# An attention and mixture-of-experts kernel: gathered rows turned on VectorE in 32x32 blocks by way of DRAM, and VectorE's sums in another order

## The chip, the cores and the metric

One core of a Trainium2 chip, all in fp32. A core has a tensor engine (TensorE, PE: matmuls and transposes, results in PSUM), a vector engine (VectorE, DVE), a scalar engine (ScalarE, ACT), GpSimd (POOL) and SyncE (SP); the last issues most DMAs here. The metric is the device time of one execution in microseconds (us), the median of the runs. For one execution there is a profile, which gives the time of every instruction on each engine and of the DMAs.

## The reference

Linear attention with decay over 4 sequences of 768 tokens and 8 heads of 64 gives a row `x` of 512 numbers for each token. Then a mixture of experts with a rule of locality: a token goes to its own best expert, or stays with the expert of the token before it.

```python
def _moe_ref(x, w_gate, w_local, w1, w2):
    B, S, D = x.shape                      # 4, 768, 512; 8 experts, F = 1024
    logits = np.einsum('bsd,de->bse', x, w_gate)
    local_gate = 1.0 / (1.0 + np.exp(-np.einsum('bsd,de->bse', x, w_local).squeeze(-1)))
    for b in range(B):
        prev_e = -1
        for s in range(S):
            fresh_e = int(np.argmax(logits[b, s]))
            if s == 0 or local_gate[b, s] < 0.5:
                e = fresh_e
            else:
                e = prev_e if prev_e >= 0 else fresh_e
            prev_e = e
            ...
            h = np.maximum(x[b, s] @ w1[e], 0.0)
            out[b, s] = p[e] * (h @ w2[e])
```

Only the expert that a token goes to is computed: per token a product of 512 by 512x1024, a relu, and a product of 1024 by 1024x512, scaled by the gate's probability.

## The kernel before

**Stages.** The attention runs in 24 steps of 128 rows; each writes its rows of `x` to `x_dram` in DRAM and the gate's logits to SBUF. DVE, PE and POOL work out which token goes to which expert and sort the tokens by expert into tiles of up to 128 tokens, each tile of one expert. The first `KA` = 5 tiles are made early, from the sequences that are done, so that they keep PE busy while the rest is sorted. What is left is done in three kinds: pairs (two full tiles of one expert), single tiles (`full`) and half tiles of 64 tokens. How many there are of each is known only as the kernel runs: `while_more` and `one_of` branch on it. In the profiled execution there are 8 pairs, 3 single tiles after the first 5, and 3 half tiles. The order is: pair 0, pair 1 (the half tiles' steps stand in these two as hooks), pair 2, the single tiles, then pairs 3 to 7.

**Rows.** `collect` gathers a tile's rows from `x_dram` into `xgt[i]` (i = 0, 1; token on the partition, 512 numbers in a row) by an indirect DMA of POOL. A product needs them the other way round, the 512 on the partitions in four groups of 128. `turned` does that: four transposes on PE (L666) into the PSUM bank `po1`, and a copy out of it, by ACT into `xp` for a pair, by DVE into `xtt[i]` for a single tile.

**Single and half tiles.** `hidden` (L674) makes the hidden layer, `output` (L680) the second product, `written` scales by the gate on DVE and scatters the rows to the output with POOL (L689).

**Pairs.** `pair` multiplies two tiles as a 2x2 block product with seven products per layer in place of eight (Strassen's scheme in Winograd's form). `product_1` (L863) is a product of layer 1, `product_2` (L868) one of layer 2. The scheme needs sums of blocks, all on DVE: `sums_of_x` over the turned rows (into `xs` and `xp`), `sums_1` over w1 (into `s1`, and one block of w1 in place), `sums_2` over w2 (into `s2`, and one block in place), four instructions each; the sums of products are in `part` (`c01`, `c10`, `c11`) for layer 1 and in `yt` and `rest` for layer 2. Products go to PSUM banks `a`, `b`, `c`; in layer 2 `c` is `pl`, and is used twice: for `hs[2]`, which the second sum of `c11` (L942) reads, and then for `h00`.

A pair prepares the next: it gathers the next pair's rows at its start (`pair_ahead`), turns the first tile after the second product of layer 2 and the second one after the fourth, adds up w1 of the next pair beside that, and makes `sums_of_x` after the sixth product. `hook(k)` calls what the caller puts between the products.

**Weights.** There are three sets in SBUF, `w1t[i]` and `w2t[i]` of 2 MB each. Pair p uses set (p+1) % 2, the half tiles set 2, the single tiles set 2 and set 1 in turn. `weights_of` loads w1 (L636) and w2 (L638) of a tile's expert by one DMA each on SP's queue; a pair loads w1 of the pair after next at its middle (after hook 6) and w2 at its end, into the set that it used itself. Before pair 2 both layers of the first single tile are loaded into set 2. The DMAs of one engine are issued in the order of its program, and a DMA that waits (for the last reader of the buffer, or a semaphore) holds up those behind it.

**Order.** In the shown part, PE, DVE and SP run in the order in which the code calls them (`manual_schedule`); ACT's and POOL's order is made by the scheduler.

Of the kernel before, what the change touches and what calls it, by code (L numbers as in the profile page):

```python
# [8 lines left out]
F32 = mybir.dt.float32  # L9
# [12 lines left out]
P = 128  # L22
# [21 lines left out]

HP = P // 2
REST = N - KA * P
PMIN = -(-(REST - E * (P + HP)) // (2 * P))
# [12 lines left out]
def kernel(  # L60
# [16 lines left out]
    dram = ctx.enter_context(tc.tile_pool(name="dram", bufs=1, space=bass.MemoryType.DRAM))  # L77
    x_dram = dram.tile([N, DM], F32, name="x_dram")
    lt = route.tile([P, NT, E + 1], F32, name="lt")
    moe = ctx.enter_context(tc.tile_pool(name="moe", bufs=2))  # L80
# [169 lines left out]
    def rows_of(s):  # L250
        px = pg.tile([P, DM], F32, name="pk1")
        for a in range(A):
            nc.tensor.transpose(px[:, P * a:P * a + P], xc[:, a, ORDER[s][0]], ident)
        if s + 1 < NS:
            xn = att.tile([P, DM], F32, name="xn", bufs=4)
        else:
            xn = act.tile([P, DM], F32, name="xn", bufs=1)
        nc.scalar.copy(xn, px)
        nc.scalar.dma_start(out=x_dram[P * s:P * s + P, :], in_=xn)
# [372 lines left out]

    def weights_of(g, i, layers=(1, 2), cond=None):
        e = expert(g)
        if 1 in layers:
            nc.sync.dma_start(out=w1t[i], in_=w1_src(e), cond=cond, cond_hint=None if cond is None else True)  # L636
        if 2 in layers:
            nc.sync.dma_start(out=w2t[i], in_=w2_src(e), cond=cond, cond_hint=None if cond is None else True)  # L638
# [76 lines left out]
    with tc.manual_schedule(engines={PE, DVE, SP}):  # L715
# [57 lines left out]
        xgh = act.tile([P, DM], F32, name="xgh", bufs=1)  # L773
        yt = act.tile([P, 2, DM], F32, name="y", bufs=1)
        xp = act.tile([P, DT, 2, P], F32, name="xp", bufs=1)
        xs = act.tile([P, 3, DT // 2, P], F32, name="xs", bufs=1)
# [89 lines left out]
    def product_2(to, a, b, new=False):  # L866
        for f in range(FT // 2):
            nc.tensor.matmul(to, lhsT=a[:, f], rhs=b[:, f], start=(new and not f), stop=(f == FT // 2 - 1),  # L868
                             skip_group_check=True)

    def pair_ahead(p):
        for i in range(2):
            ahead(KA + 2 * p + i, i)

    def pair_turned(i):
        turned(i, xp[:, :, i], nc.scalar.copy)

    def pair(p, hooks={}, next=True, load=True, cond=None):
# [12 lines left out]
        product_1(a, a1(p, 0, 0), b1(0, 0), True)  # L891
        nc.scalar.copy(c01, a)
        hook(0)
        product_1(b, s1[:, 1], xs[:, 1], True)
        tt(c10, c01, b, ALU.add)  # L895
        hook(1)
        sums_2(p, (0, 1))
        product_1(c, a1(p, 1, 0), b1(0, 1), True)
# [3 lines left out]
        tt(c11, c11, c, ALU.add)  # L902
        nc.scalar.activation(h11, c11, ACT.Relu)
        hook(3)
        sums_2(p, (2, 3))
        product_1(a, a1(p, 0, 1), b1(1, 0))
# [12 lines left out]
        nc.scalar.activation(h01, c01, ACT.Relu)  # L919
        hook(6)  # L920
        if load:
            weights_of(KA + 2 * p + 4, w_of(p), (1,), cond)
# [6 lines left out]
        nc.scalar.mul(c01, a, g1)  # L929
        hook(7)  # L930
        product_2(b, hs[:, 1], s2[:, 1], True)
        tt(hs[:, 3], h01, hs[:, 1], sub)
        stt(c10, b, g0, rest, ALU.mult, ALU.add)
        hook(8)
        if next:
            pair_turned(0)
            sums_1(p + 1, (0, 1))
        product_2(c, hs[:, 2], b2(p, 0, 1), True)
        hook(9)
        product_2(b, hs[:, 0], s2[:, 0])  # L940
        stt(c11, b, g0, rest, ALU.mult, ALU.add)
        stt(c11, c, g0, c11, ALU.mult, ALU.add)  # L942
        hook(10)
        if next:
            pair_turned(1)
            sums_1(p + 1, (2, 3))
        product_2(a, h01, b2(p, 1, 0))
        nc.scalar.mul(c00, a, g1)
        hook(11)
        product_2(c, h00, s2[:, 2])  # L950
        stt(c10, c, g0, c10, ALU.mult, ALU.add)  # L951
        scatter(KA + 2 * p, yt[:, 0])
        if next:
            sums_of_x()
        hook(12)
# [11 lines left out]
    def turned_half():  # L967
# [4 lines left out]
        nc.vector.tensor_copy(xt, pt[:, :, :HP])  # L972
        return xt

    def hidden_of_half(xt):
# [31 lines left out]
    def hooks_of_halves(n):  # L1007
# [7 lines left out]
        def steps(h):  # L1015
# [11 lines left out]
            def end():  # L1027
                output_of_half(h, now["ht"])
                if h + 1 < n:
                    weights_of(G2 + h + 1, 2)  # L1030

# [29 lines left out]
    with tc.manual_schedule(engines={PE, DVE, SP}):  # L1061
# [6 lines left out]
        hidden(0, 0, 0)  # L1068
        hidden(0, 0, 1)
        weights_of(KA + 2, w_of(1), (1,))  # L1070
        pair_turned(0)
        sums_1(0, range(4))
        output(0, 0)
        pair_turned(1)
        sums_of_x()
        written(4, 0)
        weights_of(KA + 2, w_of(1), (2,))
        weights_of(G2, 2)

# [7 lines left out]
        fulls = number(1, E + 1)  # L1087
        pair(2, {10: [lambda: ahead(G1, 0)], 12: [lambda: ahead(G1 + 1, 1)], 13: [lambda: turned(0)]}, load=False)

# [3 lines left out]
        def full(f):  # L1093

            i, w = f % 2, w_of_full(f)
            if f + 1 < E:
                if f:
                    ahead(G1 + f + 1, 1 - i)
                else:
                    weights_of(G1 + 1, w_of_full(1), cond=fulls > 1)  # L1100
            hidden(i, w, 0)
            hidden(i, w, 1)
            if f + 1 < E:
                turned(1 - i)
            output(i, w)
            written(G1 + f, i)
            if f + 2 < E:
                weights_of(G1 + f + 2, w, cond=fulls > f + 2)

# [46 lines left out]
```

## Time and profile before

| | us |
|---|---|
| runs | 478.14, 480.98, 483.45; median 480.98 |
| the profiled execution | 479.6 |
| its span, from the first instruction to the last | 477.9 |
| mean granted TensorE clock | 0.989 |

Stages of the profiled execution, in us from the start of the span:

| stretch | what | PE busy | DVE busy |
|---|---|---|---|
| 0 to 170 | attention, sorting, first tiles | 159.7 | 95.8 |
| 170 to 184 | the last of the first five tiles | 14.0 of 14 | 6.0 |
| 184 to 264 | pairs 0 and 1 with the half tiles | 76.9 of 80 | 42.5 |
| 264 to 290 | pair 2 | 26.0 of 26 | 19.7 |
| 290 to 338 | three single tiles | 43.8 of 48 | 5.3 |
| 338 to 478 | pairs 3 to 7 | 127.6 of 140 | 95.7 |

Pairs 3 to 7 start at 338.33, 364.0, 389.5, 415.0 and 440.5. An engine's name with a q (SPq) is the queue that issues for it. In a line of the timeline or the chain the first number is the start, the second the duration; `x8` counts instructions. The releaser of a wait is what came last by the semaphores.

### The profile page before, as it was taken

The page shows a single profiled execution, that of the slowest core. Times are in us where ns is not written, and L with a number is a line of the kernel's source. Part 1 is how long each engine was busy: PE and PEld are TensorE (multiplying, and loading weights), DVE is VectorE, ACT ScalarE, POOL GpSimd, SP SyncE. Part 2 cuts the span into 40 slices and gives each one's busy share as a digit, 9 for nine tenths or more (in the row PEclk, how much of TensorE's full clock was granted, in tenths as well). Part 3 has the DMA queues.
Part 4 walks back from the last instruction along what each step waited for, and adds up shares of the span by engine and source line. Part 5 has one row for each costly group of instructions (what it writes and reads, how often), then busy time and mean ns, then how long its engine had stood idle before and what let it go on. Part 6 is the DMA issues. An engine that isn't in the chain of part 4 may idle for free. (4 is left out here: it accounts for less than half of the span.)

```text
span 477.9 us, 10471 instructions
## 1 busy us (share of the span) xinstructions
PE 447.9 (94%) x4307; PEld 371.4 (78%) x4307; DVE 264.9 (55%) x515; ACT 112.4 (24%) x265; POOL 112.9 (24%) x121
## 2 busy tenths in 40 slices
PE   8898999999999998899999999989999999999990
PEld 7776887777776776868777988647799999998980
DVE  6553676762269451835473783101386868687780
ACT  3265665431100110211121130000031312121120
POOL 4574654500111200214001311101203030110200
PEclk9899999999999999999999999999999999999997
DMA  7999999996888988998990799831594838250201
GB/s 289 406 421 350 364 346 344 394 408 230 282 306 300 359 278 302 403 394 314 347 352 12 239 360 405 308 132 41 185 392 156 299 91 317 93 205 23 67 3 46
DMA packets 42241, 126.20 MB, mean 264 GB/s; under 512 B 3132, under 2 KB 3132, under 8 KB 39360
## 3 DMA queue, kind: packets, MB, share of 16 engines
q1 hardware_dynamic: 34256, 104.88, 59.7%
q0 software_dynamic: 4464, 14.16, 8.1%
q10 hardware_dynamic: 3456, 6.29, 3.5%
q8 instruction: 40, 0.66, 0.5%
q14 instruction: 25, 0.20, 0.1%
HBM read 137.91 MB, written 12.98 MB: 316 GB/s over the span
## 5 line engine op out<-in xcount | busy, mean ns | idle before, releaser
L689 POOL DMA_INDIRECT out_dram<-y,sidx x24 | 24.8, 1034 | 199.6 <-DVE y L951 98.9
L674 PEld LDWEIGHTS ps<-xt,w 128*128 128x128 f32 x512 | 58.1, 192 | 4.5 <-issue 2.6
L674 PE MATMUL ps<-xt,w 128*128 128x128 f32 x512 | 59.2, 276 | 1.3 <-DVE xt L667 1.0
L680 PE MATMUL pk<-w,h 128*128 128x512 f32 x128 | 56.3, 592 | 0.0
L651 POOL DMA_INDIRECT xg<-x_dram,gidx x27 | 30.5, 1130 | 77.7 <-PE po L666 36.8
L680 PEld LDWEIGHTS pk<-w,h 128*128 128x128 f32 x128 | 23.7, 190 | 26.8 <-issue 26.8
L198 DVE TENSOR_TENSOR sm<-ps,mask 128x512 f32<-128x512 f32 x46 | 29.6, 686 | 20.4 <-PE ps L194 20.4
L863 PE MATMUL ps<-xp,w 128*128 128x128 f32 x256 | 31.7, 276 | 2.6 <-issue 1.5
L863 PEld LDWEIGHTS ps<-xp,w 128*128 128x128 f32 x256 | 30.4, 192 | 4.5 <-issue 4.2
L863 PE MATMUL ps<-xs,s 128*128 128x128 f32 x256 | 31.3, 275 | 1.6 <-DVE part L895 1.6
L676 ACT ACTIVATE h<-ps 128x512 f32<-128x512 f32 x16 | 9.6, 597 | 94.1 <-PE ps L674 74.7
L863 PEld LDWEIGHTS ps<-xs,s 128*128 128x128 f32 x256 | 29.9, 192 | 1.8 <-DVE part L895 1.8
L169 POOL TENSOR_TENSOR qd<-inp,lamq 128x512 f32<-128x512 f32 x20 | 25.6, 1281 | 20.2 <-PE po L221 8.8
L868 PE MATMUL pk<-w,h 128*128 128x256 f32 x128 | 30.3, 379 | 0.0
L868 PE MATMUL pk<-s,hsum 128*128 128x256 f32 x128 | 30.2, 379 | 0.0
L234 PE MATMUL po<-sm,inp 128*64 128x128 f32 x384 | 27.5, 284 | 1.2 <-issue 1.1
L234 PEld LDWEIGHTS po<-sm,inp 128*64 128x64 f32 x384 | 21.3, 139 | 8.1 <-issue 6.9
L868 PEld LDWEIGHTS pk<-s,hsum 128*128 128x128 f32 x128 | 24.0, 190 | 3.1
L172 POOL TENSOR_TENSOR kd<-inp,rev 128x512 f32<-128x512 f32 x20 | 21.7, 1084 | 19.6 <-PE pk L243 10.1
L868 PEld LDWEIGHTS pk<-w,h 128*128 128x128 f32 x128 | 23.1, 190 | 2.5
L697 DVE TENSOR_SCALAR y<-pk,gate 128x512 f32<-128x512 f32 x8 | 6.0, 748 | 33.1 <-PE pk L680 27.1
L194 PE MATMUL ps<-inp 64*64 64x128 f32 (+1 forms) x736 | 21.4, 253 | 3.0 <-DMA inp<-in_qkv_dram 1.8
(244 smaller groups left out, 734.1 us busy)
## 6 DMA issues: line engine op xcount, KB each, us to landing
w<-in_w_dram SPq DMA_DIRECT2D x49, 2048.0 KB
inp<-in_qkv_dram SPq DMA_DIRECT2D x22, 1024.0 KB
x_dram<-xn ACTq DMA_DIRECT2D x24, 256.0 KB
inp<-in_qkv_dram SPq DMA_DIRECT2D x4, 512.0 KB
w<-in_w_dram SPq DMA_DIRECT2D x4, 512.0 KB
xg<-x_dram,gidx POOLq DMA_INDIRECT x27, 6.7
out_dram<-y,sidx POOLq DMA_INDIRECT x24, 6.9
xgh<-x_dram,gidx POOLq DMA_INDIRECT x3
```

The source lines that it names most:

```text
L169: nc.gpsimd.tensor_tensor(qd, x[:, 0].rearrange("p (a i) -> p a i", i=P), lamq, ALU.mult)
L172: nc.gpsimd.tensor_tensor(kd.rearrange("p (h d) -> p h d", d=DH), x[:, 2].rearrange("p (h d) -> p h d", d=DH), rev.unsqueeze(2).broadcast_ ...
L194: nc.tensor.matmul(ps[u][half, a, first:], lhsT=kt[rows, a, js], rhs=qt[rows, a, first:], start=True, stop=True, skip_group_check=True)
L198: nc.vector.tensor_tensor(sm[:, u], ps[u], mask[:, u], ALU.mult)
L234: nc.tensor.matmul(head(a, u), lhsT=vn[:, a, u], rhs=sm[:, u, a], start=(not c and a < 2), stop=True, skip_group_check=True)
L651: nc.gpsimd.indirect_dma_start(out=xg, out_offset=None, in_=x_dram[:n, :], in_offset=bass.IndirectOffsetOnAxis(ap=gidx[i][:, j:j + 1], axi ...
L674: nc.tensor.matmul(ph[:, j], lhsT=w1t[w][:, d, P * f:P * f + P], rhs=xtt[i][:, d], start=(d == 0), stop=(d == DT - 1))
L676: nc.scalar.activation(hq[half, i], ph, ACT.Relu)
L680: nc.tensor.matmul(pys[i], lhsT=hq[f // 4, i][:, f % 4], rhs=w2t[w][:, f], start=(f == 0), stop=(f == FT - 1))
L689: apart(nc.gpsimd.indirect_dma_start(out=out, out_offset=bass.IndirectOffsetOnAxis(ap=sidx[i][:, j:j + 1], axis=0), in_=y, in_offset=None, ...
L863: nc.tensor.matmul(to[:, m], lhsT=a[:, k, P * m:P * m + P], rhs=b[:, k], start=(new and not m and not k), stop=(k == 1), skip_group_check= ...
L868: nc.tensor.matmul(to, lhsT=a[:, f], rhs=b[:, f], start=(new and not f), stop=(f == FT // 2 - 1), skip_group_check=True)
```

## The change

- The gathered rows of pairs and single tiles are not turned on PE any more. SP writes `xgt[i]` to a buffer in DRAM (`xg_dram[i]`, 256 KB) and reads it back in four DMAs of 64 KB (`fetched`): quarter q of each row goes to the partitions 32q to 32q+31, with four groups of 32 tokens side by side. One transpose on DVE then turns every 32x32 block in place (`blocks_turned`). A row's element on partition 32q+j, group d, is thus number 128q + 32d + j; before, partition p of group d held number 128d + p.
- w1 has to lie in the same order. `weights_of` therefore loads w1 by four DMAs, one for each 32 partitions (0.5 MB each). Half tiles keep the turns on PE and the old order (`weights_of_half`). The first five tiles keep both too.
- In a pair, `sums_2` stands earlier (for pair 0 in one row after `c11`), the first two of `sums_1` of the next pair stand in layer 1, the last two after the first and second product of layer 2 (in pair 0 two and two there), both turns after the third, and `sums_of_x` after the fifth. The writes and reads of the next pair's rows are issued after hook 6, ahead of the load of w1.
- In pair 2 the rows of two single tiles are gathered at hook 7. A single tile turns the next one's rows at its start, gathers those of the one after next there, and fetches them at its end.
- The last step's `xn` takes a part of `part` as its buffer, so that there is room for the two tiles `xqs`.

Line numbers of the file after the change are higher by 4 at `weights_of` and by about 50 at its end.

```diff
@@ -76,6 +78,8 @@
 
     dram = ctx.enter_context(tc.tile_pool(name="dram", bufs=1, space=bass.MemoryType.DRAM))
     x_dram = dram.tile([N, DM], F32, name="x_dram")
+
+    xg_dram = [dram.tile([P, DM], F32, name=f"xg_dram{i}") for i in range(2)]
     lt = route.tile([P, NT, E + 1], F32, name="lt")
     moe = ctx.enter_context(tc.tile_pool(name="moe", bufs=2))
     rt = ctx.enter_context(tc.tile_pool(name="rt", bufs=1))
@@ -631,9 +635,13 @@
         nc.sync.dma_start(out=w2t[g % 2], in_=w2_src(e), cond=other, cond_hint=False)
 
     def weights_of(g, i, layers=(1, 2), cond=None):
+
         e = expert(g)
         if 1 in layers:
-            nc.sync.dma_start(out=w1t[i], in_=w1_src(e), cond=cond, cond_hint=None if cond is None else True)
+            rows = w1[bass.ds(e, 1)].rearrange("o (q t j) f -> q j (o t) f", q=Q, j=QP)
+            for q in range(Q):
+                nc.sync.dma_start(out=w1t[i][QP * q:QP * q + QP], in_=rows[q], cond=cond,
+                                  cond_hint=None if cond is None else True)
         if 2 in layers:
             nc.sync.dma_start(out=w2t[i], in_=w2_src(e), cond=cond, cond_hint=None if cond is None else True)
@@ -772,6 +780,7 @@
         hq.update({(f, i): act.tile([P, FT // 2, P], F32, name=f"h{f}{i}", bufs=1) for f in range(2) for i in range(2)})
         xgh = act.tile([P, DM], F32, name="xgh", bufs=1)
         yt = act.tile([P, 2, DM], F32, name="y", bufs=1)
+        xqs = [act.tile([P, DM], F32, name=f"xq{i}", bufs=1) for i in range(2)]
         xp = act.tile([P, DT, 2, P], F32, name="xp", bufs=1)
         xs = act.tile([P, 3, DT // 2, P], F32, name="xs", bufs=1)
         s1 = act.tile([P, 3, DT // 2, F // 2], F32, name="s1", bufs=1)
@@ -868,12 +877,35 @@
             nc.tensor.matmul(to, lhsT=a[:, f], rhs=b[:, f], start=(new and not f), stop=(f == FT // 2 - 1),
                              skip_group_check=True)
 
+    def rows_of_tile(g, i):
+        ahead(g, i)
+
+    def fetched(i, parts=(0, 1)):
+
+        if 0 in parts:
+            nc.sync.dma_start(out=xg_dram[i], in_=xgt[i])
+        if 1 not in parts:
+            return
+        for q in range(Q):
+            nc.sync.dma_start(out=xqs[i][QP * q:QP * q + QP].rearrange("t (c f) -> t c f", c=Q),
+                              in_=xg_dram[i].rearrange("(c t) (q f) -> q t c f", c=Q, q=Q)[q])
+
+    def blocks_turned(i, xt):
+        nc.vector.transpose(out=xt.rearrange("p d (c t) -> p c d t", t=QP),
+                            in_=xqs[i].rearrange("p (c d j) -> p c d j", d=DT, j=QP))
+
     def pair_ahead(p):
         for i in range(2):
-            ahead(KA + 2 * p + i, i)
-
-    def pair_turned(i):
-        turned(i, xp[:, :, i], nc.scalar.copy)
+            rows_of_tile(KA + 2 * p + i, i)
+
+    def pair_fetched():
+        for part in range(2):
+            for i in range(2):
+                fetched(i, (part,))
+
+    def pair_turned():
+        for i in range(2):
+            blocks_turned(i, xp[:, :, i])
 
     def pair(p, hooks={}, next=True, load=True, cond=None):
@@ -890,19 +922,25 @@
             pair_ahead(p + 1)
         product_1(a, a1(p, 0, 0), b1(0, 0), True)
         nc.scalar.copy(c01, a)
+        if p:
+            sums_2(p, (0, 1))
         hook(0)
         product_1(b, s1[:, 1], xs[:, 1], True)
         tt(c10, c01, b, ALU.add)
+        if p:
+            sums_2(p, (2, 3))
         hook(1)
-        sums_2(p, (0, 1))
         product_1(c, a1(p, 1, 0), b1(0, 1), True)
         hook(2)
         product_1(b, s1[:, 0], xs[:, 0])
         tt(c11, c01, b, ALU.add)
         tt(c11, c11, c, ALU.add)
         nc.scalar.activation(h11, c11, ACT.Relu)
+        if not p:
+            sums_2(p, (0, 1, 2, 3))
+        elif next:
+            sums_1(p + 1, (0, 1))
         hook(3)
-        sums_2(p, (2, 3))
         product_1(a, a1(p, 0, 1), b1(1, 0))
         nc.scalar.activation(h00, a, ACT.Relu)
         hook(4)
@@ -918,6 +956,8 @@
         tt(c01, c01, b, ALU.add)
         nc.scalar.activation(h01, c01, ACT.Relu)
         hook(6)
+        if next:
+            pair_fetched()
         if load:
             weights_of(KA + 2 * p + 4, w_of(p), (1,), cond)
@@ -928,30 +968,30 @@
         nc.scalar.mul(rest, a, g0)
         nc.scalar.mul(c01, a, g1)
         hook(7)
+        if next:
+            sums_1(p + 1, (2,) if p else (0, 1))
         product_2(b, hs[:, 1], s2[:, 1], True)
         tt(hs[:, 3], h01, hs[:, 1], sub)
         stt(c10, b, g0, rest, ALU.mult, ALU.add)
         hook(8)
         if next:
-            pair_turned(0)
-            sums_1(p + 1, (0, 1))
+            sums_1(p + 1, (3,) if p else (2, 3))
         product_2(c, hs[:, 2], b2(p, 0, 1), True)
         hook(9)
+        if next:
+            pair_turned()
         product_2(b, hs[:, 0], s2[:, 0])
         stt(c11, b, g0, rest, ALU.mult, ALU.add)
         stt(c11, c, g0, c11, ALU.mult, ALU.add)
         hook(10)
-        if next:
-            pair_turned(1)
-            sums_1(p + 1, (2, 3))
         product_2(a, h01, b2(p, 1, 0))
         nc.scalar.mul(c00, a, g1)
+        if next:
+            sums_of_x()
         hook(11)
         product_2(c, h00, s2[:, 2])
         stt(c10, c, g0, c10, ALU.mult, ALU.add)
         scatter(KA + 2 * p, yt[:, 0])
-        if next:
-            sums_of_x()
         hook(12)
         product_2(b, hs[:, 3], b2(p, 1, 1))
         stt(c01, b, g1, c01, ALU.mult, ALU.add)
@@ -971,6 +1011,11 @@
         xt = act.tile([P, DT, HP], F32, name="xth", bufs=1)
         nc.vector.tensor_copy(xt, pt[:, :, :HP])
         return xt
+
+    def weights_of_half(h):
+        e = expert(G2 + h)
+        nc.sync.dma_start(out=w1t[2], in_=w1_src(e))
+        nc.sync.dma_start(out=w2t[2], in_=w2_src(e))
 
     def hidden_of_half(xt):
@@ -1027,7 +1072,7 @@
             def end():
                 output_of_half(h, now["ht"])
                 if h + 1 < n:
-                    weights_of(G2 + h + 1, 2)
+                    weights_of_half(h + 1)
 
             return start, middle, turn, end
@@ -1067,15 +1112,15 @@
         ahead_half(0)
         hidden(0, 0, 0)
         hidden(0, 0, 1)
+        pair_fetched()
         weights_of(KA + 2, w_of(1), (1,))
-        pair_turned(0)
         sums_1(0, range(4))
+        pair_turned()
+        sums_of_x()
         output(0, 0)
-        pair_turned(1)
-        sums_of_x()
         written(4, 0)
         weights_of(KA + 2, w_of(1), (2,))
-        weights_of(G2, 2)
+        weights_of_half(0)
 
         def first_pairs(n):
             hooks = hooks_of_halves(n)
@@ -1085,7 +1130,14 @@
         one_of(halves, [3, 4, 2, 5, 1, 6, 0, 7, 8], "halves", first_pairs)
         weights_of(G1, 2)
         fulls = number(1, E + 1)
-        pair(2, {10: [lambda: ahead(G1, 0)], 12: [lambda: ahead(G1 + 1, 1)], 13: [lambda: turned(0)]}, load=False)
+        def rows_of_full(f):
+            rows_of_tile(G1 + f, f % 2)
+
+        def full_turned(f):
+            blocks_turned(f % 2, xtt[f % 2])
+
+        pair(2, {7: [lambda: rows_of_full(0), lambda: rows_of_full(1)], 11: [lambda: fetched(0)],
+                 13: [lambda: full_turned(0), lambda: fetched(1)]}, load=False)
 
         def w_of_full(f):
             return w_of(2) if f % 2 else 2
@@ -1094,17 +1146,17 @@
 
             i, w = f % 2, w_of_full(f)
             if f + 1 < E:
-                if f:
-                    ahead(G1 + f + 1, 1 - i)
-                else:
+                full_turned(f + 1)
+                if not f:
                     weights_of(G1 + 1, w_of_full(1), cond=fulls > 1)
+            if f + 2 < E:
+                rows_of_full(f + 2)
             hidden(i, w, 0)
             hidden(i, w, 1)
-            if f + 1 < E:
-                turned(1 - i)
             output(i, w)
             written(G1 + f, i)
             if f + 2 < E:
+                fetched(i)
                 weights_of(G1 + f + 2, w, cond=fulls > f + 2)
 
         while_more(fulls, 0, E, "full", full)
```

More of the change, by code (lines that the diff above doesn't have):

```diff
@@ L45 @@
 HP = P // 2
+Q = 4
+QP = P // Q
 REST = N - KA * P
@@ L256, in rows_of @@
         else:
-            xn = act.tile([P, DM], F32, name="xn", bufs=1)
+            xn = part[:, 0].rearrange("p f i -> p (f i)")
         nc.scalar.copy(xn, px)
```

## The prediction

> **What bounds the kernel now.** I read the busy times of the page first, then the source view of the turning line, the chain of waits over a pair in steady state, and the queues of SyncE (SP) and the DMA around the places where the change puts its transfers.
>
> ```profile
> PE 447.9 (94%) x4307; PEld 371.4 (78%) x4307; DVE 264.9 (55%) x515; ACT 112.4 (24%) x265; POOL 112.9 (24%) x121
> ```
> TensorE is busy 94% of the span of 477.9 us; a pair of tiles (25.47 us from the start of one to the next) has no gap on it. The chain from pair 3 (start S = 338.33) shows what work the change takes out (start, duration, what):
> ```profile
> 351.08 3.46 PE pk L868 x16
> 354.53 0.44 PE po L666 x4
> 354.97 1.73 PE pl L868 x8
> 356.70 1.73 PE pk L868 x8
> 358.43 0.44 PE po L666 x4
> 358.86 1.73 PE pk L868 x8
> 360.59 1.73 PE pl L868 x8
> ```
> The two groups of four turns (L666) stand on the path. So time on TensorE counts one to one, if nothing else is late. The last line is the product `c` of `h00`; it needs the second sum of `c11` on DVE (L942), because both use the bank `pl`. Without 0.87 us of turns it is due at S+21.4 (360.59 - 338.33 - 0.87).
>
> The queue of SP at pair 2 (S = 263.92) and pair 3, and the DMA in 2-us windows after a 2 MB load issued alone at 374.79 (columns: window; PE, PEld, DVE, ACT, POOL busy; clock; DMA share; GB/s):
> ```profile
> 264.11 0.37 SPq L638 DMA_DIRECT2D w<-in_w_dram  x1
> 274.30 0.37 SPq L636 DMA_DIRECT2D w<-in_w_dram  x1
> 274.87 0.38 SPq L638 DMA_DIRECT2D w<-in_w_dram  x1
> ```
> ```profile
> 376.00:378.00 2.00, 2.00 (x13) 1.82 (x13) 1.64 (x3) 0.29 (x1) 0.00 (x0) 1.00 0.84 270
> 378.00:380.00 2.00, 2.00 (x12) 1.72 (x11) 1.24 (x3) 1.35 (x3) 0.00 (x0) 1.00 1.03 418
> 380.00:382.00 2.00, 2.00 (x13) 1.80 (x11) 1.97 (x4) 0.59 (x1) 0.00 (x0) 1.00 0.84 344
> ```
> 2 x (270+418+344) GB/s is 2.06 MB, so this is the whole load: first data about 1.9 us after the issue, then 5.0 us at 418 GB/s. In pair 2 SP holds the load of the first full tile's w1 until S+10.4 (SP's waits list one of 8.8 us, for a DMA of weights), then issues 4 MB back to back.
>
> **What goes.** The page has 104 turns of 271 to 331 ns; four tiles keep theirs, so 22 x 4 go, and each group costs 0.437 us on the path (0.873 us for two): -9.6 us. Before the first full tile's output, PE waits 2.4 us for gathered rows:
> ```profile
>   DMA xg<-x_dram,gidx: 2.4, 1
> ```
> The new order gathers two full tiles earlier, at hook 7 of pair 2: -2.4. Gain: -12.0 us. The copies that go from ACT lay beside PE.
>
> **What comes, and whether it is hidden.** Per tile: one write of 256 KB, four reads of 64 KB into 32 partitions each, one block turn on DVE. None of the turns in blocks, and no DMA that fills 32 partitions, is in this trace. Nearest rows for the block turn: DVE copies and sums of 128x512, 0.69 us; 128x1024, 1.22. I take 0.69, from 0.42 (the 128x256 copy) to 1.22.
>
> *A w1 load in four quarters of 32 partitions* is the disputed price. Call it f times 5.0 us. Bounds: 1 (same bytes and 4 KB rows) to 4 (a quarter of the partitions takes a quarter of the rate). The geometric middle is 2; I take 1.7, a bit nearer to the whole load, the only measured row. Below 1 is excluded: its middle window already shows a DMA share of 1.03.
>
> [...] No row here shows a transfer into 32 partitions.
>
> *Steady pairs.* Gathers issue at S+2.9 and S+4.3 (366.92 and 368.27, pair 4 at 364.0) and land 6.7 us later, S+11.0. Write: 1.25 us for 512 KB at 418 GB/s and 1 for issue and landing, S+13.2. Eight reads: 2.6 to issue (0.326 each, the ACT queue's issue row) + 1.9 + 0.3, S+18.0. DVE gets there at S+18.2 (354.84 + 0.48 - 338.33, + 1.22 for the last sum of weights); two turns 1.4 and two sums 1.0 end at S+20.6 against 21.4. So 0; at 1.22 a turn, +0.2 a pair. Bound: reads 2 us late make that 0.8 + 1.4 at most. DVE has room: 19.2 of 25.5 us busy. The sums of weights are reordered, not added. On SP the writes wait for the gathers, and w1 of the pair after next is queued behind them: issued at S+15.8 instead of S+10.8 (374.79), there at S+17.7+5f, S+26.2 at f = 1.7; DVE adds it up from the middle of the next pair, some 8 us later, which hides that (at f = 4, S+37.7, no longer: +3 a pair). On POOL the gathers keep their place in a pair; in pair 2 two of them go ahead of its scatters, which nobody waits for.
>
> *Pair 2.* The writes and reads of pair 3's rows stand on SP's queue behind the 4 MB above, and this queue's transfers run in order. Issue S+10.4, + 1.9, + 0.6 (shared with a gather), + 5f + 5 (w1, w2), + 1.25 (the writes), + 1 landing = S+20.2+5f. Reads + 4.8: S+25+5f. Second turn and two sums, 1.7: S+26.7+5f, against 21.4. PE stalls 5.3 + 5f: 10.3 us at f = 1, 13.8 at 1.7, 15.3 at 2, 25.3 at 4. Before, these rows were in SBUF at S+16 (273.27 + 6.7) and needed no SP.
>
> *Pair 3.* Its 4 MB issue at S+1.2 (339.56) and pair 4's rows follow: S+1.2 + 1.9 + 1.25 (gathers beside) + 5f + 5 + 2.25 + 4.8 + 1.7 = S+18.1+5f. Stall 1.7 / 5.2 / 6.7.
>
> *Pair 0.* All four sums of w2 now stand in one row on DVE behind the second sum of `c11` (L902), which ends at S+8.8 in pair 3 (346.48 + 0.69 - 338.33): + 4 x 1.24, + 3 x 0.69 (`c10`, `hs[0]`, `hs[1]`) + 0.6 (a relu on ACT between) = S+16.4, against S+14.5 when PE comes to `hs[1]` (half of the first line of the chain above, 351.08 + 1.73): +1.9 (0 to 2.5).
>
> *First full tile.* Gather 6.7, write, reads and turn in a row, behind weights; the wait for `xt` (1.0 now) grows by 1 to 2.9; taken 1 at f = 1, else 2.
>
> *Half tiles in pair 1*: their w1 keeps its layout, but waits behind two others in quarters: landing at 213.6 + 10f against a need at 226.6: 0 / 4 / 7. *Third full tile*, w1 in quarters behind another load: 0 / 4 / 7. *Rows of pair 0*: 0 (-1 to +2); PE stood there for 1.5 us before.
>
> The sum at f = 1.7: -12.0 + 13.8 + 5.2 + 1.9 + 2 + 4 + 4 = +18.9. At f = 1: -12.0 + 10.3 + 1.7 + 1.9 + 1 = +2.9. At f = 2: -12.0 + 15.3 + 6.7 + 1.9 + 2 + 7 + 7 = +27.9. At f = 4: -12.0 + 25.3 + 16.7 + 1.9 + 2 + 27 + 27 = +87.9.
>
> The profiled execution took 479.6 us (477.9 of span and 1.7 around). The median of the runs is 480.98, 1.4 more. So f = 1.7 gives 498.5, 500 on the median's scale; f = 1 gives 482.5, or 484; f = 2 gives 507.5, or 509; f = 4, 569.
>
> **Rivals.**
> *Faster: the rows pass the weights.* If the small writes and reads of pairs 2 and 3 are not held behind the 4 MB (the transfers of one queue share the engines, or the load of w1 is issued some 9 us earlier because the wait at SP goes with the new order), no pair stalls. Then it is -12.0 + 1.9 = -10.1: 469.5, or 471. The point that decides: pair 3's rows in SBUF by S+19.0 of pair 2 (21.4 less 1.4 and 1.0). For it speaks that SP's 10.2 us gap is one single wait; against it, that the writes stand after both weights in the order of SP, and can't issue before S+16 (gather) in any case, so reads end at S+23 at the best; then 4 us of stall are left, and it is 475.
> *Quarters cost nothing (f = 1):* 484. For it: bytes and row lengths are as before, and the middle window moves 418 GB/s over all engines. Against: each quarter goes to a quarter of the partitions.
> *DVE as the end of each pair:* turns at 1.22 us and reads 2 us late: 18.0 + 2 + 2.44 + 1.0 - 21.4 = 2.0 a pair, eight pairs 16; at f = 1 it is 484 + 16 = 500, with half of the delay 492. For it: nothing lies between turn and product but two sums. Against: 0.8 us of slack and 6.3 us of idle time in a pair.
> *It doesn't do what it says:* the turns leave PE by name in the diff, 22 groups; I give this nothing.
>
> **How the numbers follow.** Chances: f from 1.3 to 2, 0.48 (its own range 488 to 510); f near 1, 0.22 (480 to 489; 0.12 of it within 1%, 0.10 above); rows pass the weights, 0.17 (467 to 477; 0.15 below -1%, 0.02 within); f above 2, 0.06 (510 to 570); DVE at the end, 0.07 (490 to 500). About 1% (476 to 486) is what a measurement here can tell from no change. Faster 0.15, the same 0.14, slower 0.71. A range from 474 to 520 leaves out some 0.10 below (most of the pass-the-weights case) and 0.06 above.
>
> **What the profile after would show.** L666 x16 instead of x104, PE busy about 438 us. A stall of PE at the product `c` of `h00` in pair 2, released by DVE, which in turn waits for a DMA into the fetched rows; a smaller one in pair 3; none in pairs 4 to 6. A w1 load whose DMA windows show about 250 GB/s (f = 1.7) or 418 (f = 1). Block turns of about 0.69 us. The waits of L674 for the half and full tiles' weights show which of the +4 terms hold. I am wrong if pair 3's rows land by S+19 of pair 2, or if the stalls come in steady pairs, each the same.

## The result, and the profile after

The changed kernel takes 538.13 us (median of 6 runs, 534.37 to 539.37) against 481.33 for the kernel before on the same chip: a ratio of 1.117, 95% interval 1.111 to 1.123. Slower was right; 500, with a range up to 520, was not. The profiled execution took 537.35 us, its span is 535.6. Medians and ranges here are over all runs of a kernel, while ratios and intervals leave out a few slow executions at a lower clock (one each of e2, e3 and e12, and some of the kernel before).

The busy times of the page, as shown of before:

```profile
PE 452.7 (85%) x4219; PEld 371.3 (69%) x4219; DVE 276.9 (52%) x533; ACT 102.4 (19%) x247; POOL 113.4 (21%) x122
```

TensorE has 88 instructions fewer, and yet is busy 4.8 us longer: its instructions are slower. It also stands still for far longer, 82.9 us of the span in place of 30.0 (span less busy time). The granted clock in 40 slices, first before, then, with the DMA share, after:

```profile
PEclk9899999999999999999999999999999999999997
```
```profile
PEclk9899999999999978996999966997995999999997
DMA  8999999968889799799969975978287969695311
```

Before, the mean clock was 0.989; now it is 0.936, with dips that follow the waits. The turning line and the line that took its place (the source view of the one, the view of the fetched rows' tile for the other):

```profile
L674 PE MATMUL po<-ident,xg x16: 271/272/331, 115.3 to 162.4; 128*128 128x128 f32 x16
```
```profile
L894 DVE STREAM_TRANSPOSE xp<-xq x18: 666/711/714, 187.2 to 518.0; 128x512 f32<-128x512 f32 x18
L894 DVE STREAM_TRANSPOSE xt<-xq x4: 669/707/712, 332.0 to 377.4; 128x512 f32<-128x512 f32 x4
  DMA xq<-xg_dram: 62.4, 13
```

So the change does what it says: 104 turns became 16, and a block turn takes 0.71 us where 0.69 was taken. But DVE stood still for 62.4 us before such turns. What TensorE waited for, from the view of the waits (engine, line, releaser: us in total, times, longest):

```profile
PE pl L877 <- DVE y L985: 19.5, 4, 16.4
PE pk L877 <- DVE hsum L954: 13.5, 3, 10.7
PE pr L1024 <- DMA w<-in_w_dram: 9.4, 1, 9.4
PE ps L682 <- DMA w<-in_w_dram: 5.5, 1, 5.5
PE ps L872 <- DVE xp L894: 4.5, 1, 4.5
PE ps L872 <- DVE part L929: 4.2, 1, 4.2
```

The longest wait of the first line is the product `c` of `h00` in pair 2, as forecast; that of the second is in pair 3, but released by a hidden sum, not by the rows; the third is a half tile's weights, the fourth the third single tile's. The price of a w1 load in quarters can be read in 2-us windows after the four quarters issued from 414.26 (columns as in the prediction):

```profile
418.00:420.00 2.00, 2.00 (x11) 1.77 (x10) 1.92 (x5) 0.41 (x1) 0.00 (x0) 1.00 1.02 199
420.00:422.00 2.00, 2.00 (x11) 1.74 (x11) 0.91 (x2) 0.06 (x1) 0.00 (x0) 1.00 1.05 221
422.00:424.00 2.00, 2.00 (x16) 1.90 (x15) 0.95 (x2) 0.00 (x0) 1.02 (x1) 1.00 1.05 203
```

The DMA engines are as busy as they were with the whole load (share 1.02 to 1.05 against 1.03), and move half as much: some 208 GB/s (the mean of 199, 221 and 203) in place of 418. So f is 2.0, not 1.7. The engines aren't idle for want of work; the load takes twice as long (2 MB at 208 GB/s is 10 us, at 418 it was 5.0), and while it lasts the engines show no free time. That is the line to look at: a high share with a low rate.

Where the 57.7 us of span went, stage by stage (start of pair 0, then the length of each stage, from the first matmul of one to the first of the next; columns three to six are differences to before). The third and fifth columns are the prediction's own terms, put in the stage that they belong to, with the turns that leave it:

| stage | before | forecast at f = 2 | after | forecast at f = 1 | e1_one_load (f = 1) |
|---|---|---|---|---|---|
| until pair 0 | 183.9 | -0.9 | +4.2 | -0.9 | +0.9 |
| pair 0 | 37.7 | +1.0 | +7.1 | +1.0 | +3.2 |
| pair 1 | 42.3 | +6.1 | +11.1 | -0.9 | +6.1 |
| pair 2 | 27.1 | +14.0 | +19.3 | +9.0 | +16.2 |
| three single tiles | 47.4 | +5.3 | +4.2 | -2.7 | -3.9 |
| pair 3 | 25.6 | +5.8 | +13.0 | +0.8 | +5.1 |
| pairs 4 to 7 and the end | 114.0 | -3.5 | -1.3 | -3.5 | -2.9 |
| sum | 477.9 | +27.9 | +57.7 | +2.9 | +24.7 |

### The profile page after: what moved, and what is told of

Same layout as the page of the kernel before. It is cut to its first block, busy times and chain, and to the rows that moved or that the text cites. A ratio compares the mean times of both kernels' runs of the same rounds, so it can differ in the third digit from the quotient of the medians.

```text
span 535.6 us, 10655 instructions
## 1 busy us (share of the span) xinstructions
PE 452.7 (85%) x4219; PEld 371.3 (69%) x4219; DVE 276.9 (52%) x533; ACT 102.4 (19%) x247; POOL 113.4 (21%) x122
## 5 line engine op out<-in xcount | busy, mean ns | idle before, releaser
L682 PEld LDWEIGHTS ps<-xt,w 128*128 128x128 f32 x512 | 60.2, 198 | 10.7 <-issue 10.0
L682 PE MATMUL ps<-xt,w 128*128 128x128 f32 x512 | 61.4, 282 | 7.1 <-DMA w<-in_w_dram 5.5
L877 PE MATMUL pk<-s,hsum 128*128 128x256 f32 x128 | 32.3, 398 | 13.5 <-DVE hsum L954 13.5
L688 PEld LDWEIGHTS pk<-w,h 128*128 128x128 f32 x128 | 23.7, 190 | 26.8 <-issue 26.8
L202 DVE TENSOR_TENSOR sm<-ps,mask 128x512 f32<-128x512 f32 x46 | 29.6, 685 | 19.3 <-PE ps L198 19.2
L872 PE MATMUL ps<-xp,w 128*128 128x128 f32 x256 | 33.2, 285 | 5.9 <-DVE xp L894 4.5
L872 PE MATMUL ps<-xs,s 128*128 128x128 f32 x256 | 33.7, 289 | 4.2 <-DVE part L929 4.2
L872 PEld LDWEIGHTS ps<-xs,s 128*128 128x128 f32 x256 | 32.4, 206 | 4.4 <-DVE part L929 4.4
L877 PE MATMUL pl<-s,h 128*128 128x256 f32 x64 | 17.3, 418 | 19.5 <-DVE y L985 19.5
L894 DVE STREAM_TRANSPOSE xp<-xq 128x512 f32<-128x512 f32 x18 | 12.4, 702 | 39.6 <-DMA xq<-xg_dram 39.6
L173 POOL TENSOR_TENSOR qd<-inp,lamq 128x512 f32<-128x512 f32 x20 | 25.6, 1280 | 19.6 <-PE po L225 7.0
L877 PEld LDWEIGHTS pl<-s,h 128*128 128x128 f32 x64 | 12.9, 207 | 22.9 <-DVE y L985 21.1
```

The lines of the kernel that those rows point to most:

```text
L173: nc.gpsimd.tensor_tensor(qd, x[:, 0].rearrange("p (a i) -> p a i", i=P), lamq, ALU.mult)
L202: nc.vector.tensor_tensor(sm[:, u], ps[u], mask[:, u], ALU.mult)
L682: nc.tensor.matmul(ph[:, j], lhsT=w1t[w][:, d, P * f:P * f + P], rhs=xtt[i][:, d], start=(d == 0), stop=(d == DT - 1))
L688: nc.tensor.matmul(pys[i], lhsT=hq[f // 4, i][:, f % 4], rhs=w2t[w][:, f], start=(f == 0), stop=(f == FT - 1))
L872: nc.tensor.matmul(to[:, m], lhsT=a[:, k, P * m:P * m + P], rhs=b[:, k], start=(new and not m and not k), stop=(k == 1), skip_group_check= ...
L894: nc.vector.transpose(out=xt.rearrange("p d (c t) -> p c d t", t=QP), in_=xqs[i].rearrange("p (c d j) -> p c d j", d=DT, j=QP))
```

## The experiments

**One load of w1 again.** The whole change, but without quarters:

```diff
-            rows = w1[bass.ds(e, 1)].rearrange("o (q t j) f -> q j (o t) f", q=Q, j=QP)
-            for q in range(Q):
-                nc.sync.dma_start(out=w1t[i][QP * q:QP * q + QP], in_=rows[q], cond=cond,
-                                  cond_hint=None if cond is None else True)
+            nc.sync.dma_start(out=w1t[i], in_=w1[bass.ds(e, 1)].rearrange("o (p t) f -> p (o t) f", p=P), cond=cond,
+                              cond_hint=None if cond is None else True)
...
-                            in_=xqs[i].rearrange("p (c d j) -> p c d j", d=DT, j=QP))
+                            in_=xqs[i].rearrange("p (c j d) -> p c d j", d=DT, j=QP))
```

> The changed kernel, but w1 comes in one DMA over 128 partitions: partition p takes rows 4p to 4p+3, and the block turn reads every fourth element of a quarter row, so that rows and weights agree. Theory A (the quarters into 32 partitions halve the rate of a w1 load, 10 us instead of 5, and most of the loss follows from that): w1 back at 5 us, the waits for weights at the third single tile (5.5 us) and a half tile (9.4) gone or below 2, the wait of DVE for w1 in the middle of pair 3 down by 5 from 11.1, PE's stall in pair 2 down by 5 from 16.4; about 505 us. Rival B (the place of the rows' transfers on SP's queue and DVE's new order make the loss): 525 to 538. The block turn, 0.70 us now, may cost more with a stride.

504.49 us (ratio to before 1.047, 1.040 to 1.054). Theory A's time held: 33.6 of the 56.8 us come back. The wait for the third single tile's weights is gone, that of the half tile is 4.1, and pair 3's wait for a hidden sum 2.2. Pair 2's wait fell less than expected, from 16.4 to 14.0. The stride has a price, in the groups of the DVE view:

```profile
L892 DVE STREAM_TRANSPOSE xp<-xq 128x512 f32<-128x512 f32 x18 | 19.3, 1087 | 34.2 <-DMA xq<-xg_dram 34.2
L892 DVE STREAM_TRANSPOSE xt<-xq 128x512 f32<-128x512 f32 x4 | 4.3, 1089 | 12.3 <-DMA xq<-xg_dram 12.3
```

1.09 us a turn with every fourth element, 0.70 with elements in a row. What is left, 24.7 us of span, isn't the quarters; the slower turn has a part in it that wasn't separated.

**Quarters alone, and what makes them slow.** Four kernels, each the kernel before with only the w1 loads of `weights_of` cut up (this includes the half tiles', which the change leaves whole):

```diff
-            nc.sync.dma_start(out=w1t[i], in_=w1_src(e), cond=cond, cond_hint=None if cond is None else True)
+            for p in parts:
+                nc.sync.dma_start(out=w1t[i][p], in_=w1_src(e)[p], cond=cond, cond_hint=None if cond is None else True)
```

where the parts are `[32 * q:32 * q + 32]` for four q in e2 (quarters in a row), `[:, t]` for four t in e3 (all partitions, one of the four row groups each), `[r::4]` for four r in e9 (every fourth partition) and `[64 * h:64 * h + 64]` for two h in e10 (halves).

> The kernel before, only that each w1 load of pairs, single and half tiles is four DMAs of 32 partitions, with the rows where they were. Theory A: each takes 10 us; waits at the half tiles and the third single tile of 4 to 9 us each, the pairs have room: 489 to 497 us. Rival B: 481 within 2.

> The kernel before, each of those w1 loads as four DMAs of 128 partitions (one of the four row groups each). Theory A (the partitions are what counts): 481 within 2. Rival C (four DMAs in place of one, their issues and semaphores, cost the time): as much as with 32 partitions, 489 to 497.

> The kernel before with each w1 load in four DMAs of 32 partitions as in e2_before_quarters, but each takes every fourth partition, so that it is spread over all 128. [...] Rival G (a DMA with 32 rows of partitions is slow wherever they lie): as e2_before_quarters, 520 to 526.

> The kernel before with each w1 load in two DMAs of 64 partitions next to each other. [...] Rival G (the rate follows the number of partitions): 64 partitions at 0.75 to 1 of the full rate, 483 to 500.

| kernel | us | ratio to before, 95% interval |
|---|---|---|
| e2, 4 x 32 partitions in a row | 523.91 | 1.085, 1.078 to 1.093 |
| e3, 4 x 128 partitions | 486.55 | 1.012, 1.007 to 1.016 |
| e9, 4 x 32 partitions, spread | 494.59 | 1.028, 1.022 to 1.033 |
| e10, 2 x 64 partitions in a row | 517.85 | 1.077, 1.072 to 1.081 |

The windows over a w1 load in a late pair, where nothing else is on the way, first of the halves, then of the spread quarters:

```profile
418.00:420.00 2.00, 2.00 (x13) 1.82 (x12) 2.00 (x3) 0.59 (x1) 0.00 (x0) 1.00 1.03 200
420.00:422.00 2.00, 2.00 (x12) 1.72 (x11) 1.24 (x2) 0.00 (x0) 0.00 (x0) 1.00 1.02 211
```
```profile
394.00:396.00 2.00, 2.00 (x11) 1.70 (x10) 1.25 (x3) 1.35 (x3) 0.00 (x0) 1.00 1.03 412
396.00:398.00 2.00, 2.00 (x13) 1.81 (x12) 2.00 (x3) 0.59 (x1) 0.00 (x0) 1.00 0.98 385
```

Same DMA share, 200 to 211 GB/s against 412. So it is not the number of partitions in a DMA (64 are as slow as 32, and 32 spread ones as fast as 128), but which ones: the halves 0 to 63 and 64 to 127, and the four quarters of 32 in a row, run at half rate (some 208 GB/s in the quarters of the changed kernel). Nor is it the side of DRAM: a quarter of the changed kernel and a fourth of e3 both read 0.5 MB that lie in one piece, and e3's load moves up to 395 GB/s in a 2-us window. Why parts in a row are slow isn't shown by these runs; the price is measured, 418 to some 208 GB/s, 2.0.

The times weren't all as expected. e3 and e9 move weights at the full rate, and yet cost 6 and 14 us. In both, PE waits ahead of pair 2 for a load of weights, 2.7 and 10.0 us, while SP sends four DMAs for each load. What ties pair 2 to that load wasn't settled; theory C may have a share here. And e2 costs some 41 us (by the ratio) where two separate waits of 4 to 9 us were expected: one load's 5 us more were weighed against that load's own slack, but the loads share one queue, and in pair 0 the DMA share was 0.93 already (in e2 it is 1.04, at 232 GB/s).

**The order of the transfers.** On e1_one_load:

```diff
-        weights_of(G1, 2)
         fulls = number(1, E + 1)
...
-        pair(2, {7: [lambda: rows_of_full(0), lambda: rows_of_full(1)], 11: [lambda: fetched(0)],
-                 13: [lambda: full_turned(0), lambda: fetched(1)]}, load=False)
+        pair(2, {7: [lambda: weights_of(G1, 2, (1,)), lambda: rows_of_full(0), lambda: rows_of_full(1)], 11: [lambda: fetched(0)],
+                 13: [lambda: full_turned(0), lambda: fetched(1), lambda: weights_of(G1, 2, (2,))]}, load=False)
```

> The kernel of e1_one_load (504.5 us), only that in pair 2 the first single tile's w1 is issued after the writes and reads of pair 3's rows, and its w2 at the pair's end. Theory A (rows held behind 4 MB on SP's queue make pair 2's stall of 14.0 us): that stall falls to about 4 (the second gather lands only at S+16 of the pair), and with it some 2 us of half clock go; the first single tile then waits some 5 us for its rows, which now stand behind w1; in all about 497 us. Rival (the chain write, read, turn takes that long by itself, wherever it stands): the stall stays above 10 and the time at 503 or more.

498.31 us (1.035, 1.028 to 1.041). Theory A held: the wait in pair 2 is 3.7 in place of 14.0. The single tiles now wait 3.0, 2.7 and 0.6 where only the first waited, 1.6; so of the 10 us 6 are left.

**The order of DVE's sums**, also on e1_one_load:

```diff
-        if not p:
-            sums_2(p, (0, 1, 2, 3))
-        elif next:
+        if next and p and p != 3:
             sums_1(p + 1, (0, 1))
...
-            sums_1(p + 1, (2,) if p else (0, 1))
+            sums_1(p + 1, (0, 1) if p in (0, 3) else (2,))
...
-            sums_1(p + 1, (3,) if p else (2, 3))
+            sums_1(p + 1, (2, 3) if p in (0, 3) else (3,))
```

(In pair 0 the sums of w2 go back behind hooks 1 and 3.)

> The kernel of e1_one_load, only that in pair 0 the sums of w2 stand where they stood before the change (two after the second product, two after the fourth), and in pair 3 the first two sums of the next w1 come after layer 1 in place of its middle. Theory E (DVE runs in order, so a sum that waits for weights holds up the sums of the hidden layer behind it): the waits of PE for the hidden sums, 1.26 us in pair 0 and 2.17 in pair 3, go; 501 us. Rival: those waits have another source, 504 within 2.

503.57 us (1.046, 1.039 to 1.052): not to be told from 504.49. The two waits did go; the rest of 0.5 in pair 3 has another releaser. But the next wait of pair 3, for the rows, grew from 3.3 to 4.7, and a later wait of pair 0, at the product `c` of `h00`, of 2.1 appeared. The mechanism is real, and was worth nothing here, where a later wait stands in the same pair.

**Both orders with the quarters kept:**

> The changed kernel, its quarters kept, with both changes of order: in pair 2 rows ahead of the first single tile's weights (e5), sums of pairs 0 and 3 later (e6). With w1 in one load the two were worth 6 and 1 us. Theory H (with the quarters the DMA is busy nearly all the time from pair 0 to the single tiles, so an order can only move a wait): 533 to 538 us. Rival (each wait is its own, from its place in a queue): pair 2's stall and pair 3's 10.7 us go, 515 to 525.

538.29 us, 0.3 above theory H's range and far from the rival's. Against the changed kernel, pair 2 is 10.4 us shorter (35.9 in place of 46.4), and the single tiles are 13.0 longer (64.5 in place of 51.5), since they now wait for their rows (8.8) and for weights (8.6, 3.4 and 3.0). But its reason holds only in part: the DMA share is 0.94 and 0.93 in pairs 0 and 1 and 0.74 to 0.83 from pair 2 to pair 3, so the engines are not full there. In the changed kernel SP waits 81.3 us in all for rows to be written before it reads them back; how much of the time that makes wasn't tried.

**The clock.** The changed kernel with matmuls that nobody reads in two of PE's waits:

```diff
+        if p == 3:             # ahead of the product of hs[1]; 44 in e7
+            warm = pg.tile([P, A, P], F32, name="po1")
+            for _ in range(30):
+                nc.tensor.matmul(warm[:, 0], lhsT=ident, rhs=ident, start=True, stop=True)
         product_2(b, hs[:, 1], s2[:, 1], True)
...
+        if p == 2:             # 68 in e7
+            warm = pg.tile([P, A, P], F32, name="po1")
+            for _ in range(50):
+                nc.tensor.matmul(warm[:, 0], lhsT=ident, rhs=ident, start=True, stop=True)
         product_2(c, h00, s2[:, 2])
```

> The changed kernel with matmuls that nobody reads in two of PE's waits: 50 of 128x128 in pair 2 ahead of the product that waits 16.4 us, 30 in pair 3 ahead of the one that waits 10.7. Theory D (a PE that stands still is granted half the clock, and keeps it for some us after work resumes): the products behind these waits go back from 3.78, 2.31 and 3.78, 2.85 us to 1.73 each; 5.8 us less, about 532. Rival: the slow products have another cause (shared transfers): 538 within 2.

> The changed kernel with 68 and 44 matmuls (0.227 us each, as measured) where e4_filled_wait had 50 and 30, so that PE stands still for under 2 us in pairs 2 and 3. Theory D': the clock goes to half once PE stood still for some 4 us and stays there for about 4 after it resumes; with the rest under 2 us the products behind run at 1.73 each and the time falls by some 5 us from 538. Rival: they stay at 2 us or more each, 538.

538.65 and 539.57 us: no gain. The changed kernel's windows about the end of the wait in pair 2 (PE resumes at 325.65), then those of e7_filled_longer (PE resumes at 324.94, after 1.75 us without work):

```profile
324.00:326.00 2.00, 0.35 (x1) 0.35 (x2) 1.93 (x5) 0.00 (x0) 0.00 (x0) 0.50 0.13 36
326.00:328.00 2.00, 2.00 (x6) 1.55 (x6) 1.15 (x3) 0.00 (x0) 0.00 (x0) 0.50 0.66 226
```
```profile
324.00:326.00 2.00, 1.06 (x5) 0.95 (x6) 1.93 (x6) 0.00 (x0) 0.00 (x0) 1.00 0.33 96
326.00:328.00 2.00, 2.00 (x11) 1.77 (x10) 0.93 (x3) 0.00 (x0) 0.26 (x1) 1.00 0.47 167
```

The slow products behind a wait are the clock (0.50, 6 instructions in 2 us, against 1.00 and 11), and filling the wait keeps it up. In e4, where 5.5 and 4.6 us stayed empty, it still fell (mean 0.955, in e7 0.963). But the time doesn't follow: e7's third single tile waits 7.8 us for its weights where it waited 5.5, and pairs 4 and 5 wait 1.7 and 2.0 for DVE (0 and 0.6 without the filling). The faster products only reach the next transfer sooner. So the clock of 0.936 is a sign of waiting here, and in these two places no cause of its own. The length of a wait alone doesn't decide whether the clock falls: it did behind the 4.6 us of e4 and didn't behind the 1.75 of e7, but in e1_one_load the first product behind waits of 3.06 and 2.76 us in pair 0 took 3.58 and 3.40 us, where such a product takes 1.95 at the full clock, while the one behind a wait of 3.26 us in pair 3 ran at full speed (eight instructions in 1.99 us, 1.89 for the next eight).

**Where it pays.** Block turns only where the transfers have room:

> The kernel before with the block turns only in pairs 3 to 7 (rows of pairs 4 to 8), where nothing large stands in front of the rows: w1 everywhere in one DMA with four rows to a partition, PE's own turns on every fourth column, in pair 3 the next w2 behind the rows. Theory A: ten groups of turns (4.4 us) go and no stall takes their place; 476 to 478 us. Rival (the way by DRAM or DVE delays each pair): stalls of over 0.5 us in pairs 4 to 7, 481 or more.

> The kernel before with block turns in pairs 4 to 7 alone (rows of pairs 5 to 8; their w1 in one DMA, four rows to a partition); all else as before, PE's own turns contiguous again. Theory A: pairs of 24.6 us in place of 25.5 for four pairs, as pairs 5 and 6 had in e8_part_blocks; 3.5 us less, 477 to 479. Rival (pair 4 pays it back with a wait for its rows, as with 1.7 us there): 480 to 482.

The second one, against the kernel before (the functions of the rows' way and the order of the sums in a pair with blocks are those of e1_one_load, only that the last two sums of the next w1 follow the turns and `sums_of_x` keeps its old place):

```diff
+            src = w1[bass.ds(e, 1)].rearrange("o (p t) f -> p (o t) f", p=P) if blocks else w1_src(e)
+            nc.sync.dma_start(out=w1t[i], in_=src, cond=cond, cond_hint=None if cond is None else True)
...
+            weights_of(KA + 2 * p + 4, w_of(p), (1,), cond, blocks=p >= 3)
...
-                                                                load=PMIN + k + 2 < PMAX, cond=more > k + 2))
+                                                                load=PMIN + k + 2 < PMAX, cond=more > k + 2, blocks=True))
```

e8_part_blocks took 483.23 us (1.005, 1.001 to 1.009), no gain. The chain of its pair 5 shows that the turns are off the path there:

```profile
405.43 3.46 PE pk L872 x16
408.88 1.73 PE pl L872 x8
410.61 3.45 PE pk L872 x16
414.06 1.73 PE pl L872 x8
415.79 1.73 PE pk L872 x8
```

Pairs 5 and 6 take 24.59 and 24.60 us in place of 25.47, the whole 0.87. Elsewhere it was given back: pair 4 has a wait of 1.7 (for DVE, in the pair after the one in which weights were put behind the rows), the single tiles take 1.8 us longer, and PE's own turns are slower: with every fourth column their loads of 128x128 take 211 ns in place of 141 (medians).

e12_blocks_from_4 leaves all that out: 477.53 us (474.5 to 481.99, 9 runs), 0.992 of the kernel before, 0.988 to 0.995. That is 3.2 us less by the medians and 4.1 by the ratio, as much as four pairs of turns are worth (3.5): its pairs 4 to 6 take 24.59, 24.59 and 24.60 us, without a wait. It is a gain of under 1%, and the only version here that beats both kernels.

## Why the prediction was wrong, point by point

- **The gain was right.** 22 groups of turns left PE; where no transfer is late, a pair is shorter by 0.87 us (e8, e12). The block turn (0.71 for 0.69) and the order of the queue were right too: the writes of pair 3's rows, issued from 299.93 behind 4 MB, kept SP waiting for 13.1 us, while in e5, without 4 MB ahead of them, the reads issued 2.1 us after the first write (286.45 and 284.35); the first read of pair 3's rows was forecast at S+20.2+5f, S+30.2 at f = 2, and it issued at S+30.15 (316.55 - 286.40).
- **f was mis-sized:** 1.7 was the author's estimate, below the middle of 1 and 4 since the whole load was the only measured row; no run shows it, and the windows show 2.0 (418 GB/s for the whole load, some 208 for the quarters). The error is worth 9 of the 38 us by the prediction's own sum (27.9 less 18.9).
- **The step that failed is the sum of separate waits, with nothing for slower products.** Of the 57.7 us, 52.9 are idle time of TensorE and 4.8 busy time; the sum at f = 2 has +37.5 (its waits less the 2.4) and -9.6. So it lacks 15.4 us of waits and 14.4 of slower products. The second is a term that it doesn't have: "PE busy about 438 us" came out as 452.7, with a clock of 0.82 to 0.93 in the stages from pair 0 to pair 3. Of the waits, 6.3 come ahead of pair 0, where "Rows of pair 0: 0" stood (4.5 of them for these rows), and 4.0 in pair 3 (see its term below). The terms of the half tiles and of the third single tile were near, 9.4 and 5.5 for 7 each.
- **These are shares of the time, not prices**, and that is what adding up one wait at a time missed: with the quarters a better order took 10.4 us out of pair 2 and put 13.0 into the single tiles (e11), and the full clock in two places brought nothing (e7). The quarters cost 33.0 us of span (57.7 less 24.7) where the sum had 25.0 (27.9 less 2.9). So most of what it lacks is there with whole loads too: e1 has 25.0 of idle time and -0.3 of busy time against +12.5 and -9.6 at f = 1, that is 12.5 of waits (4.1 for a half tile's weights, put at 0; 4.4 more in pair 2) and 9.3 of slower products. Of this only the order in pair 2 was tried (e5, 6 us); the rest is read from the traces, and its causes stay open.
- **Pair 3's term had the wrong mechanism.** It was priced as rows behind 4 MB, 6.7 at f = 2. What stopped PE was a sum of the next w1, moved up into layer 1: DVE waited for that load, and the hidden sums stood behind it. The chain of the changed kernel shows it:

```profile
391.71 12.38 DMA w<-in_w_dram
...
404.22 1.24 DVE s L850
405.48 1.23 DVE w L850
...
407.99 0.70 DVE hsum L953
408.72 0.70 DVE hsum L954
...
409.47 3.78 PE pk L877 x8
```

  The prediction called the sums "reordered, not added" and priced the order in pair 0 alone. At full rate the same wait is 2.2 us (e1), and taking it away brings nothing (e6).
- **Pair 2 was right in kind and nearly in size:** 16.4 for 15.3 at f = 2. The eight reads took longer than the 4.8 us given: from the first issue to the second block turn 7.45 (324.00 - 316.55), with a gather of POOL beside them; issuing them alone took SP 3.64 us, not 2.6.
- **Left out altogether:** the clock, behind the slower products above. Taking it away changed nothing in the two places that were tried; elsewhere it wasn't tried.
- **The rivals.** The rows didn't pass the weights; quarters at no price were refuted by e2. DVE did not end every pair: it is 52% busy, and pair 4 has no wait. But pairs 5 and 6, forecast without a stall, wait 0.56 and 1.45 us for it, since its second turn waits for the fetched rows. The measured time lies in the range given to f above 2 (510 to 570, chance 0.06), but not by its condition: f is 2.0.
- **Open:** the waits at pair 0's start. DVE stands still for 8.1 us ahead of L929 for nothing that the profile shows, PE 4.2 for it (1.65 before, 2.8 with whole loads); this wasn't tried.

## What to carry to other kernels

Before a load is cut into groups of partitions, ask which partitions each part fills: 32 or 64 in a row ran at half the rate of 128 or of 32 spread ones (199 to 221 GB/s against 418 and 385 to 412), with the DMA engines shown as fully busy (share 1.02 to 1.05). And where transfers stand one behind the other and the DMA share of a stretch is high (0.77 to 0.95 from pair 0 to pair 3 here), a longer transfer can't be priced by its own slack: add up the transfer time of the whole stretch first, and allow for a TensorE that runs slower behind the long waits (clock 0.50 behind the 16.4 us of pair 2, 0.82 to 0.93 over the stages from pair 0 to pair 3). Here the turns that left a full TensorE paid what they cost (0.87 us a pair in e8 and e12), but only in the stages in which their replacement found room.

## What the runs showed of the hardware that wasn't expected

- A load into 64 partitions in a row was as slow as one into 32: 200 to 211 GB/s (e10) and 199 to 221 (the changed kernel), against 385 to 412 for 32 spread over all 128 (e9).
- In the traces here, from 184 us on, TensorE's products ran slower behind every wait of 4.1 us or more (clock 0.50 in the windows of the changed kernel) and behind none of under 1.9 us; in between they did either (in e1 they kept their speed behind one of 3.26 us, and lost it behind one of 2.76). In the changed kernel the clock was below 1.00 in six stretches between 186 and 416 us, of 3.6 to 17.2 us each, the end of the wait included.
- A block turn of 128x512 took 0.70 us from elements in a row (the changed kernel), 1.09 from every fourth (e1).
